# Attention and a three-way maxout layer on one core: two head pairs a turn, half-array matmuls in three stretches

## The chip, the core and the metric

The kernel runs on one core of a Trainium2 chip. The metric is the device time of one execution in microseconds (us). A core has a matmul engine (PE, with PEld for its weight loads), a vector engine (DVE), an activation engine (ACT), a general engine (POOL), and a queue engine (SP) that issues most DMAs. Each engine runs its own instructions in order and waits on semaphores for the others.

## What is computed

Inputs are q, k and v of 8 batches, 12 heads, 448 positions, 64 numbers a head, and four weights of 768 x 768, all float32.

```python
scores = scale * np.matmul(q, k.transpose(0, 1, 3, 2))     # scale = 1/8
m = np.max(scores, axis=-1, keepdims=True)
e = np.exp(scores - m)
attn = e / (np.sum(e, axis=-1, keepdims=True) + np.exp(-m) + 1e-09)
x = np.matmul(attn, v)                  # then (batch, position, head*64): 3584 x 768
h = np.maximum(np.maximum(x @ w1, x @ w2), x @ w3)
out = h @ w_out                         # 3584 x 768
```

The kernel leaves out the maximum m (it cancels): a row's weights are exp(score) over one plus their sum.

## The kernel before

Heads are worked on in pairs: NP = 48 pairs, NPAIR = 6 to a batch. The main loop (L452) does one pair an iteration, `p = it`, and finishes the pair before, `prev = it - 1`. P_DMA = 12 is the first pair of batch 2; from there the transposes of q and k are done by DMA instead of PE.

Of the 448 keys of a head, 384 are three chunks of 128 and 64 are left. The steps of a pair:

- `load` (L83): two DMAs (`q`, `k`, `v` each) from DRAM into one of NRAW = 3 raw buffers, each of HB = 3 pairs. They are issued on SP, as are DMA transposes and output stores, in program order.
- `cast_qk` (L165) on DVE to float16; `scale_v` (L191) on POOL; `transposes` (L204) into `qkT`, with an SP DMA from pair 12 on.
- `scores(p, c)` (L235): for chunk c, two matmuls with 64 rows, one for each head, each on one half of the PE array (tile `64*128`, side by side). Their result takes one of two buffers of the pool `ps_s`. `exp_scores` (L248) on ACT empties it. `scores_last` (L251) treats the 64 left keys of both heads in one full-array matmul, `exp_last` (L264) empties it into `eL`.
- `av_main` (L269): six full-array matmuls, `av_last` (L282): two half-array matmuls that end the sums. The results `avs` hold values and sums of weights, in the pool `ps_av` of two banks.
- `reciprocals` (L293) on ACT: two logarithms and one exponential. `normalize` (L302) on DVE for each head writes `xT` and frees an `av` bank.

When a batch has all six pairs normalized, `batch_done` (L435) appends its layer work to a queue: 18 `up` groups (six matmuls of 448 columns each, emptied by DVE into `hT`) and six or eight `op` groups (six matmuls of 384 columns, emptied by DVE into an output tile, one tile for two groups; three output tiles; stored by SP). `group()` (L443) takes one from the queue. Groups are spread between the attention steps; they use the pool `ps_u` of two banks. `n_groups` of 3 to 5 an iteration is worked out from the length of the queue.

There is no scheduler: the order written is the order on each engine (`manual_schedule`, L73). In an iteration from 12 on, before the change:

```python
cast_qk(it + 2); transposes(it + 2); scale_v(it + 1)
exp_scores(p, c, scores(p, c))                     # c = 0, 1
group()
avs = [av_main(prev, hh) for hh in range(2)]; av_last(prev, avs)
stp = scores(p, 2); stl = scores_last(p)
rb = reciprocals(prev, avs); exp_scores(p, 2, stp); exp_last(p, stl)
group(); normalize(prev, 0, avs, rb); group(); normalize(prev, 1, avs, rb)
...
load(it + 5, 1)
```

Batch 0 and 1 have orders of their own. Batch 0 fills PE with idle matmuls, and its weights (`load_weight`, L144) are loaded by POOL DMAs issued in iterations 3 to 8. In iterations 7 to 10, `casts(it + 1)` and PE transposes of the next pair stand inside the iteration.

Of the kernel before, what the change touches and what calls it, by code (L numbers as in the profile page):

```python
# [10 lines left out]
FP32 = mybir.dt.float32  # L11
FP16 = mybir.dt.float16
AF = mybir.ActivationFunctionType
# [8 lines left out]
def kernel(  # L22
# [11 lines left out]
    nc = tc.nc  # L34

    B, H, S, D = q.shape
    NTOK, DM = out.shape
    DFF = moe_w1.shape[1]
    NB = 3
# [24 lines left out]
    small = ctx.enter_context(tc.tile_pool(name="small", bufs=2))  # L64
    xt_pool = ctx.enter_context(tc.tile_pool(name="xt", bufs=2))
    ht_pool = ctx.enter_context(tc.tile_pool(name="ht", bufs=2))
    out_pool = ctx.enter_context(tc.tile_pool(name="outp", bufs=3))

    ps_s = ctx.enter_context(tc.tile_pool(name="ps_s", bufs=2, space=bass.MemoryType.PSUM))
    ps_av = ctx.enter_context(tc.tile_pool(name="ps_av", bufs=2, space=bass.MemoryType.PSUM))  # L70
# [2 lines left out]
    ctx.enter_context(tc.manual_schedule())  # L73


    NRAW = 3
    HB = NPAIR // 2
    raw = [
        [cpool.tile([128, 2 * HB, NB + 1, D], FP32, name=f"{n}in{i}") for n in "qkv"]
        for i in range(NRAW)  # L80
# [18 lines left out]
    load(1, 1, "qk")  # L99
    load(0, 1, "v")  # L100
    load(2, 1, "qk")
    load(1, 2, "v")
    load(3, 1, "qk")
    load(4, 2, "q")
    load(3, 1, "v")
    load(4, 2, "k")
    load(4, 2, "v")

# [4 lines left out]
    nc.vector.memset(raw[2][0][64:128, 0:2, NB, :], 0.0)  # L113
    load(NPAIR, 1, "qk")

    ident16 = cpool.tile([128, 128], MMDT, name="ident16")
# [34 lines left out]
    qkTs = {}  # L151
# [96 lines left out]
    def exp_scores(p, c, stp):  # L248
        nc.scalar.activation(out=eT[:, p % 2, c], in_=stp[:, :, 0:S], func=AF.Exp, scale=scale)  # L249

    def scores_last(p):  # L251

        stl = ps_s.tile([128, 2, 512], FP32, tag="s", name="stl")
        qkT, q0, k0 = qkTs.pop(p)
        nc.tensor.matmul(  # L255
            out=stl[:, 0, 0:S],
            lhsT=qkT[:, k0 + NB * 128 : k0 + NB * 128 + 128],
            rhs=qkT[:, q0 : q0 + S],
            start=True,
            stop=True,  # L260
        )
        return stl

    def exp_last(p, stl):  # L264
        nc.scalar.activation(out=eL[:, p % 2], in_=stl[:, 0, 0:S], func=AF.Exp, scale=scale)  # L265
# [177 lines left out]
    def group():  # L443
        if queue:
            queue.pop(0)()
# [3 lines left out]
    casts(0)  # L449
    transposes(0)  # L450
    keep_busy(3)
    for it in range(NP + 1):  # L452
        p = it if it < NP else None
# [12 lines left out]
        if it in (3, 4):  # L466
            load_weight(0, it - 3)
        if it in (5, 6, 8):
            load_weight((5, 6, 8).index(it) + 1)
        if it < NPAIR:  # L470

            casts(it + 1)
            for c in range(2):
                exp_scores(p, c, scores(p, c))
            if prev is None:
                keep_busy(3)
                exp_scores(p, 2, scores(p, 2))
                transposes(1)
                exp_last(p, scores_last(p))
            else:  # L480
                den, av = (ps_av.tile([128, 512], FP32, tag="av", name=n) for n in ("den", "av"))
                sums_main(prev, den, 1)
                stp = scores(p, 2)
                sums_main(prev, av, 0)
                stl = scores_last(p)
                sums_last(prev, den, 1)
                sums_last(prev, av, 0)
                exp_scores(p, 2, stp)
                exp_last(p, stl)
                rb = reciprocals_one(den)  # L490
                transposes(it + 1)
            if it < NPAIR - 1:
                keep_busy(3)
            else:

                ups = [up_open()]
                up_part(ups[0], 0, 0, 0, range(3))
                av5 = ps_s.tile([128, 2, 512], FP32, tag="s", name="av5")
                sums_main(p, av5[:, 1], 1)
                sums_main(p, av5[:, 0], 0)  # L500
                sums_last(p, av5[:, 1], 1)
                sums_last(p, av5[:, 0], 0)
                rb5 = reciprocals_one(av5[:, 1])
            if prev is not None:
                normalize_one(prev, av, rb)
            if it == NPAIR - 1:
                normalize_one(p, av5[:, 0], rb5)
                batch_done(0)
        elif it == NPAIR:
            exp_scores(p, 0, scores(p, 0))  # L510

            up_part(ups[0], 0, 0, 0, (3,))
            ups.append(up_open())
# [12 lines left out]
            exp_scores(p, 2, scores(p, 2))  # L526
            exp_last(p, scores_last(p))
            group()
            transposes(it + 1)
            group()  # L530
        else:
            late = it + 1 < P_DMA
            if not late:

                if it + 2 < NP:
                    cast_qk(it + 2)
                    transposes(it + 2)
                if it + 1 < NP:
                    scale_v(it + 1)
            if p is not None:  # L540
                for c in range(2):
                    exp_scores(p, c, scores(p, c))
# [5 lines left out]
            if p is not None:  # L548
                stp = scores(p, 2)
                stl = scores_last(p)  # L550
            rb = reciprocals(prev, avs)
            if p is not None:
                exp_scores(p, 2, stp)
                exp_last(p, stl)
# [6 lines left out]
            if it % NPAIR == 0:  # L561
                batch_done(prev // NPAIR)
# [41 lines left out]
```

## Time and profile before

| | |
|---|---|
| median of 3 runs | 367.58 us (367.43 to 367.74) |
| profiled execution | 367.07 us |
| its span, first to last instruction | 365.3 us |
| PE busy | 357.4 us, 98% |
| DVE busy | 243.4 us, 67% |
| ACT busy | 221.1 us, 61% |
| clock granted to PE | 0.999 of full |
| DMA moved | 58.61 MB, 160 GB/s on average |

The span is what the profile's times are counted in; the runs' time holds some 1.8 us more around it. PE's busy time is made of matmuls that overlap: one takes about 0.35 us from start to modelled end while the next starts 0.19 us after it. So what is read for PE is the distance from start to start. A timeline row names start, length, engine, line, operation, result and operands, the part of the array (128*128 or 64*128), the shape, and the count of equal instructions in a row; what stands in brackets is the idle time before it and who ended it.

### The profile page before, as it was taken

Reading aid. Unit: us, or ns where it says so; the run is one execution under the profiler, and the core shown is the slowest. Engines: PE = TensorE matmul, PEld = TensorE weight load, DVE = VectorE, ACT = ScalarE, POOL = GpSimd, SP = SyncE. Lnnn points to the kernel's source line nnn. Section 1 sums busy time; section 2 is a strip of 40 time slices with the busy share of each in tenths; the row PEclk is TensorE's granted clock in tenths of the full one; section 3 lists DMA queues with packets and bytes.
Section 4 is the critical chain, followed back from the end, with each engine's and each line's share of the span. In section 5 each row is a group of like instructions: output and inputs, shape, how many; then the busy total and the mean of one; then the engine's idle time right before and its main releaser. Section 6 shows DMA issues by size and latency. Waiting matters only on the chain.

```text
span 365.3 us, 6122 instructions
## 1 busy us (share of the span) xinstructions
PE 357.4 (98%) x2086; PEld 163.9 (45%) x2086; DVE 243.4 (67%) x521; ACT 221.1 (61%) x335; POOL 53.6 (15%) x159
## 2 busy tenths in 40 slices
PE   8999999999999999999999999999999999999995
PEld 3434444444444444444444444444444444445552
DVE  4474777876578677577657867757666776555553
ACT  4996476765666766666567666666566766651000
POOL 4263112211211211211121121121112112000000
PEclk9999999999999999999999999999999999999999
DMA  5999997668667888849764896758675673005006
GB/s 151 229 234 229 233 247 211 155 177 214 161 180 182 208 184 154 195 107 185 182 173 122 178 200 164 175 133 214 159 174 137 165 208 83 5 2 131 2 0 172
DMA packets 87951, 58.61 MB, mean 160 GB/s; under 512 B 43504, under 2 KB 84464, under 8 KB 87920
## 3 DMA queue, kind: packets, MB, share of 16 engines
q1 hardware_dynamic: 83632, 53.18, 59.7%
q0 software_dynamic: 3920, 4.72, 7.5%
q10 hardware_dynamic: 368, 0.33, 0.4%
q8 instruction: 16, 0.26, 0.3%
q14 instruction: 15, 0.12, 0.1%
HBM read 42.47 MB, written 11.01 MB: 146 GB/s over the span
## 4 chain that ended last, share of the span: by engine, by line
PE 91%; ACT 2%; DMA 2%; DVE 2%; issue 1%; SPq 0%; DVEq 0%
PE up L356 44%; PE op L390 15%; PE av L273 13%; PE stp L239 8%; PE stl L255 4%; PE av L285 3%; DMA kin<-in_k_dram 2%; PE busy L349 2%; ACT eT L249 1%; PE trT L221 1%; PE trT L226 1%; PE av L316 1%; DVE qkT L233 1%; DVE o_sb L415 0%; DVE qk L183 0%
## 5 line engine op out<-in xcount | busy, mean ns | idle before, releaser
L356 PE MATMUL up<-xT,w 128*128 128x448 f16 x864 | 175.3, 353 | 0.7 <-DVE xT L307 0.4
L249 ACT ACTIVATE eT<-stp 128x896 f16<-128x896 f32 x144 | 125.5, 910 | 53.3 <-PE stp L239 53.3
L356 PEld LDWEIGHTS <-w 128*128 128x128 f16 x864 | 81.7, 98 | 81.7 <-issue 12.5
L372 DVE TENSOR_TENSOR hT<-hT,up 128x448 f16<-128x448 f16 x96 | 59.6, 621 | 52.1 <-PE up L356 51.1
L157 POOL TENSOR_SCALAR vst<-vin 128x384 f16<-128x384 f32 x132 | 43.1, 338 | 255.2 <-issue 159.2
L298 ACT ACTIVATE lnd<-av 64x448 f32<-64x448 f32 x84 | 45.3, 539 | 49.0 <-PE av L285 48.0
L390 PE MATMUL op<-w,hT 128*128 128x384 f16 x336 | 59.3, 326 | 0.0
L273 PE MATMUL av<-eT,vst 128*128 128x448 f16 x252 | 54.5, 352 | 0.0
L307 DVE TENSOR_TENSOR xT<-av,rb 64x448 f16<-64x448 f32 x84 | 51.8, 617 | 1.4
L239 PE MATMUL stp<-qkT 64*128 64x448 f16 x288 | 44.1, 353 | 1.5 <-DVE qkT L233 0.7
L370 DVE CAST hT<-up 128x448 f16<-128x448 f32 x48 | 29.8, 624 | 22.9 <-PE up L356 22.2
L415 DVE TENSOR_SCALAR o_sb<-op 128x384 f32<-128x384 f32 (+1 forms) x56 | 30.8, 550 | 20.0 <-PE op L390 19.0
L390 PEld LDWEIGHTS <-hT 128*128 128x128 f16 x336 | 31.6, 98 | 24.7 <-issue 4.0
L273 PEld LDWEIGHTS <-vst 128*128 128x128 f16 x252 | 24.7, 98 | 22.4
L184 DVE CAST qk<-kin 128x384 f16<-128x384 f32 x47 | 25.7, 548 | 1.1 <-DMA kin<-in_k_dram 0.7
L265 ACT ACTIVATE eL<-stl 128x448 f16<-128x448 f32 x48 | 25.9, 539 | 0.0
L299 ACT ACTIVATE rb<-lnd 128x448 f32<-128x448 f32 x42 | 24.2, 576 | 1.3
L239 PEld LDWEIGHTS <-qkT 64*128 64x128 f16 x288 | 11.0, 94 | 23.2 <-issue 16.5
L419 ACT ACTIVATE o_sb<-op 128x192 f32<-128x192 f32 x1 | 0.3, 331 | 30.2 <-DVE o_sb L415 30.2
L189 DVE CAST qk<-kin 64x64 f16<-64x64 f32 x94 | 17.5, 187 | 1.3
L255 PE MATMUL stl<-qkT 128*128 128x448 f16 x48 | 17.4, 362 | 0.0
L285 PE MATMUL av<-eL,vst 64*128 64x448 f16 x84 | 15.2, 359 | 0.0
(50 smaller groups left out, 117.7 us busy)
## 6 DMA issues: line engine op xcount, KB each, us to landing
out_dram<-o_sb SPq DMA_DIRECT2D x54, 192.0 KB, 2.8
qin<-in_q_dram SPq DMA_DIRECT2D x46, 128.0 KB, 3.0
kin<-in_k_dram SPq DMA_DIRECT2D x45, 128.0 KB, 2.9
vin<-in_v_dram SPq DMA_DIRECT2D x44, 128.0 KB, 2.9
kin<-in_k_dram SPq DMA_DIRECT2D x46, 96.0 KB, 2.7
qin<-in_q_dram SPq DMA_DIRECT2D x45, 96.0 KB, 2.7
vin<-in_v_dram SPq DMA_DIRECT2D x44, 96.0 KB, 2.8
w<-in_moe_w_dram POOLq DMA_DIRECT2D x2, 1152.0 KB, 17.1
```

Source lines behind the costliest of these rows:

```text
L157: nc.gpsimd.tensor_scalar(out=out, in0=in_, scalar1=LAMBDA, scalar2=1.0, op0=ALU.mult, op1=ALU.mult)
L239: nc.tensor.matmul(out=stp[:, hh, 0:S], lhsT=qkT[hh * D : hh * D + D, k0 + c * 128 : k0 + c * 128 + 128], rhs=qkT[hh * D : hh * D + D, q0 ...
L249: nc.scalar.activation(out=eT[:, p % 2, c], in_=stp[:, :, 0:S], func=AF.Exp, scale=scale)
L255: nc.tensor.matmul(out=stl[:, 0, 0:S], lhsT=qkT[:, k0 + NB * 128 : k0 + NB * 128 + 128], rhs=qkT[:, q0 : q0 + S], start=True, stop=True,)
L273: nc.tensor.matmul(out=av[:, 0:S], lhsT=vst[:, p % VB, hh * NB + c, (1 - hh) * D : (3 - hh) * D], rhs=eT[:, p % 2, c, hh, :], start=(c == ...
L298: nc.scalar.activation(out=lnd[mine], in_=avs[hh][other, 0:S], func=AF.Ln, bias=1.0)
L307: nc.vector.tensor_tensor(out=xTs[b][mine, j, :], in0=avs[hh][mine, 0:S], in1=rb[mine], op=ALU.mult)
L356: nc.tensor.matmul(out=ps[:, 0:S], lhsT=w_sb[i][:, dc, ts(fc, 128)], rhs=xTs[b][:, dc, :], start=(dc == 0), stop=(dc == NDC - 1),)
L370: nc.vector.tensor_copy(out=h, in_=ps[:, 0:S])
L372: nc.vector.tensor_tensor(out=h, in0=h, in1=ps[:, 0:S], op=ALU.max)
L390: nc.tensor.matmul(out=ps[:, 0:NW], lhsT=hTs[sb][:, fc, ts(t, 128)], rhs=wout_sb[:, fc, ts(nh, NW)], start=(fc == 0), stop=(fc == NFC - 1),)
L415: nc.vector.tensor_scalar(out=o_sb[:, cs], in0=src, scalar1=1.0 / LAMBDA, scalar2=None, op0=ALU.mult)
```

## The change

Pairs 12 to 47 are done two a turn in a new loop; pairs 0 to 11 keep their iterations. In a turn, half-array matmuls stand in three stretches: `av_last(p-1)` with `scores(p, 0)` and `(p, 1)`; `scores(p, 2)` with `scores(p+1, 0)`; `av_last(p)` with `scores(p+1, 1)` and `(p+1, 2)`. The left keys of both pairs go into one `ps_s` buffer (`scores_last2`), emptied by one activation of 128 x 896 (`exp_last2`). `ready` casts, transposes and scales between the groups, twice a turn. Eight to ten groups are taken a turn.

Raw inputs have four buffers of two pairs; from pair 8 on they are loaded two pairs at a time, six DMAs a turn. For pairs 8 and 9 the load is issued in iteration 5, behind small memsets of the buffer. Output tiles are five. In the first loads, v of pair 1 goes alone and v of pairs 2 and 3 together.

```diff
-    out_pool = ctx.enter_context(tc.tile_pool(name="outp", bufs=3))
+    out_pool = ctx.enter_context(tc.tile_pool(name="outp", bufs=5))
...
-    NRAW = 3
-    HB = NPAIR // 2
+    NRAW = 4
+    HB = 2
...
-    load(1, 2, "v")
+    load(1, 1, "v")
     load(3, 1, "qk")
     load(4, 2, "q")
-    load(3, 1, "v")
+    load(2, 2, "v")
...
+    def scores_last2(p):
+        stl = ps_s.tile([128, 2, 512], FP32, tag="s", name="stl")
+        for n in range(2):
+            qkT, q0, k0 = qkTs[p + n]
+            nc.tensor.matmul(
+                out=stl[:, n, 0:S],
+                lhsT=qkT[:, k0 + NB * 128 : k0 + NB * 128 + 128],
+                rhs=qkT[:, q0 : q0 + S],
+                start=True,
+                stop=True,
+            )
+        return stl
+
+    def exp_last2(stl):
+        nc.scalar.activation(out=eL, in_=stl[:, :, 0:S], func=AF.Exp, scale=scale)
...
-    for it in range(NP + 1):
+    for it in range(P_DMA):
...
-        first = {3: 1, 4: 2}.get(it)
-        if first is not None:
-            hs = slice(2 * first, 2 * first + 2)
-            nc.vector.memset(raw[2][0][64:128, hs, NB - 1 : NB + 1, :], 0.0)
-            if first == 1:
-                load(NPAIR, 1, "v")
-            load(NPAIR + first, 1)
+        if it == 3:
+            nc.vector.memset(raw[NRAW - 1][0][64:128, 2:4, NB - 1 : NB + 1, :], 0.0)
+            load(NPAIR, 1, "v")
+            load(NPAIR + 1, 1)
+        if it == 5:
+            for t in raw[0]:
+                nc.vector.memset(t[64:128, :, NB - 1, 0:1], 0.0)
+            load(NPAIR + 2, 2)
...
-        for n in range(NPAIR + HB, 2 * NPAIR) if it == NPAIR else (it + 5,):
-            if it >= NPAIR and n < NP:
-                load(n, 1)
+        if it >= NPAIR and it % 2 == 0:
+            load(it + 4, 2)
+
+    def ready(p):
+        if p < NP:
+            cast_qk(p)
+            transposes(p)
+        if p - 1 < NP:
+            scale_v(p - 1)
+
+    avs = [av_main(P_DMA - 1, hh) for hh in range(2)]
+    for p in range(P_DMA, NP, 2):
+        left = max(len(queue) - LEFT, 0)
+        to_next = (NPAIR - p % NPAIR) // 2
+        n_groups = 8 if p % NPAIR == 0 else max(8, min(10, -(-left // to_next)))
+        av_last(p - 1, avs)
+        stps = [scores(p, c) for c in range(2)]
+        rb = reciprocals(p - 1, avs)
+        for c in range(2):
+            exp_scores(p, c, stps[c])
+        group()
+        normalize(p - 1, 0, avs, rb)
+        group()
+        normalize(p - 1, 1, avs, rb)
+        if p % NPAIR == 0:
+            batch_done(p // NPAIR - 1)
+        group()
+        exp_last2(scores_last2(p))
+        ready(p + 2)
+        for _ in range(n_groups - 7):
+            group()
+        stps = [scores(p, 2), scores(p + 1, 0)]
+        exp_scores(p, 2, stps[0])
+        exp_scores(p + 1, 0, stps[1])
+        group()
+        ready(p + 3)
+        if p + 4 < NP:
+            load(p + 4, 2)
+        avs = [av_main(p, hh) for hh in range(2)]
+        av_last(p, avs)
+        stps = [scores(p + 1, c) for c in (1, 2)]
+        rb = reciprocals(p, avs)
+        for c in (1, 2):
+            exp_scores(p + 1, c, stps[c - 1])
+        group()
+        for hh in range(2):
+            normalize(p, hh, avs, rb)
+        group()
+        group()
+        avs = [av_main(p + 1, hh) for hh in range(2)]
+    av_last(NP - 1, avs)
+    rb = reciprocals(NP - 1, avs)
+    group()
+    normalize(NP - 1, 0, avs, rb)
+    group()
+    normalize(NP - 1, 1, avs, rb)
+    batch_done(B - 1)
     while queue:
         group()
```

More of the change, by code (lines that the diff above doesn't have):

```diff
@@ L112 @@
         nc.vector.memset(raw[i][0][64:128, :, NB, :], 0.0)
-    nc.vector.memset(raw[2][0][64:128, 0:2, NB, :], 0.0)
+    nc.vector.memset(raw[NRAW - 1][0][64:128, 0:2, NB, :], 0.0)
     load(NPAIR, 1, "qk")
@@ L451 @@
     keep_busy(3)
-    for it in range(NP + 1):
-        p = it if it < NP else None
+    for it in range(P_DMA):
+        p = it
         prev = it - 1 if it > 0 else None
@@ L533 @@
             if not late:
[L535 to L542, printed above, removed]
+                cast_qk(it + 2)
+                transposes(it + 2)
+                scale_v(it + 1)
+            for c in range(2):
+                exp_scores(p, c, scores(p, c))
             group()
@@ L547 @@
             av_last(prev, avs)
-            if p is not None:
-                stp = scores(p, 2)
-                stl = scores_last(p)
+            stp = scores(p, 2)
+            stl = scores_last(p)
             rb = reciprocals(prev, avs)
-            if p is not None:
-                exp_scores(p, 2, stp)
-                exp_last(p, stl)
+            exp_scores(p, 2, stp)
+            exp_last(p, stl)
             if late:
@@ L560 @@
             normalize(prev, 1, avs, rb)
-            if it % NPAIR == 0:
-                batch_done(prev // NPAIR)
             if it + 2 == P_DMA:
@@ L567 @@
                 group()
-        for n in range(NPAIR + HB, 2 * NPAIR) if it == NPAIR else (it + 5,):
-            if it >= NPAIR and n < NP:
-                load(n, 1)
+        if it >= NPAIR and it % 2 == 0:
[14 more added lines that the diff above has]
+        rb = reciprocals(p - 1, avs)
+        for c in range(2):
+            exp_scores(p, c, stps[c])
[36 more added lines that the diff above has]
+    batch_done(B - 1)
     while queue:
```

## The prediction

> **What bounds the kernel.** I read the page's totals first, then busy time by stage, then the timeline of one pair on each engine, and the DMA answers for 28 to 50 us.
>
> Busy totals of the page:
>
> ```profile
> span 365.3 us, 6122 instructions
> PE 357.4 (98%) x2086; PEld 163.9 (45%) x2086; DVE 243.4 (67%) x521; ACT 221.1 (61%) x335; POOL 53.6 (15%) x159
> ```
>
> Stages, from pair 12 to pair 47 (columns: stretch, length, busy time by engine, clock, DMA):
>
> ```profile
> 73.10:323.00 249.90, 249.46 (x1414) 112.51 (x1415) 174.73 (x372) 163.81 (x248) 32.26 (x102) 1.00 0.68 162
> ```
>
> In this stage PE never lacks work: 249.46 of 249.90 us at full clock. A kernel can be shorter there only if the same matmuls take fewer start-to-start steps. One pair of heads on PE, from one `scores` to the next (start, length, name, count):
>
> ```profile
> 214.27 0.55 PE L239 MATMUL stp<-qkT 64*128 64x448 f16 x4
> 214.75 1.31 PE L356 MATMUL up<-xT,w 128*128 128x448 f16 x6
> 215.90 1.30 PE L273 MATMUL av<-eT,vst 128*128 128x448 f16 x6
> 217.13 0.36 PE L285 MATMUL av<-eL,vst 64*128 64x448 f16 x2
> 217.33 0.35 PE L239 MATMUL stp<-qkT 64*128 64x448 f16 x2
> 217.61 0.36 PE L255 MATMUL stl<-qkT 128*128 128x448 f16 x1
> 217.81 3.57 PE L356 MATMUL up<-xT,w 128*128 128x448 f16 x18
> 221.31 0.55 PE L239 MATMUL stp<-qkT 64*128 64x448 f16 x4
> ```
>
> The tail gives the plain step of a full-array matmul: 108 of them from 332.24 until the next kind starts at 352.78, 0.190 us each (0.189 without a 0.1 us stall among them):
>
> ```profile
> 332.24 20.70 PE L356 MATMUL up<-xT,w 128*128 128x448 f16 x108
> ```
>
> Two half-array matmuls (`64*128`) run side by side; two of `av` to two of `stp` is 217.13 to 217.33, 0.20 for a couple. The cycle is 7.04 us: 31 full matmuls make 5.86, four couples 0.80, and 0.38 is left for its two half-array stretches, 0.19 each. Locally: 18 `up` take 3.50 where 3.40 is due, 0.10 for entering; the `stp` x4 take 0.48 where 0.40 is due, 0.08 for leaving.
>
> **The change, part by part.**
>
> *Fewer stretches.* Two pairs had four stretches (`stp` x4; `av` x2 + `stp` x2; twice); a turn has three (6, 4 and 6 matmuls). Every matmul remains. Turns 12 to 46 are 18, so 18 stretches go: 18 x 0.19 = -3.4 us, all on PE, which bounds the stage. Ends: -3.2 (with 0.190 a step) and -3.6 (0.20 a stretch). The Trainium skill, "TensorEngine Tiling (Array Packing)", Key Properties, says that changing the tiling mode drains the array. A whole drain would be an estimate of 0.164 (a matmul's 353 ns less the 189 step) at both ends, 18 x 0.33 = 5.9; the row's 0.19 says the drain is partly covered, and I keep the row.
>
> *Old stalls that go.* At 80.17 the sixth `up` waits for batch 1's last normalize: due at 78.69 + 5 x 0.19 = 79.64, so 0.5 us. In turn 12 three `op` groups and the `stl` couple come before that `up`, which then starts 4.0 us after `av_last`, its sixth matmul at 4.9; normalize ends near 4.2. The `stp` at 73.10 take 0.73 instead of 0.48, a wait for ACT of 0.25 that goes too. Sum -0.75.
>
> *ScalarE inside a turn.* Its rows:
>
> ```profile
> 217.53 1.10 ACT L298 ACTIVATE lnd<-av 64x448 f32<-64x448 f32 x2 [1.13 <-PE av L285]
> 218.66 0.58 ACT L299 ACTIVATE rb<-lnd 128x448 f32<-128x448 f32 x1
> 219.15 0.90 ACT L249 ACTIVATE eT<-stp 128x896 f16<-128x896 f32 x1
> 219.94 0.54 ACT L265 ACTIVATE eL<-stl 128x448 f16<-128x448 f32 x1
> ```
>
> ACT starts 0.40 after `av_last`, needs 1.62 for the reciprocals, 0.80 a score tile, 0.90 to the end. With only two score buffers the tight place is the second stretch: its second couple needs `exp_last2` done. Counted from the turn's first `av_last`, with `op` groups (0.163 a matmul): three couples and leaving, 0.68; three groups, 3.62; `stl` couple, 4.00, its last result 4.16; group 4, 4.97; entering, 5.07; second couple at 5.27. `exp_last2` (taken as the 0.91 of the same 128x896 shape) starts 0.04 later and ends at 5.12, and PE sees it at 5.17: covered by 0.1; with `up` groups by 0.25. Before the third stretch and before `av_main(p+1)` the cover is 0.2 to 1 us. Price 0; if the cover fails, each 0.1 us is 1.8 us in all.
>
> *VectorE casts.* `ready` puts the casts of a pair between two group evacuations, in the middle of the turn. Rows of an odd batch:
>
> ```profile
> 215.21 0.55 DVE L178 CAST qk<-qin 128x384 f16<-128x384 f32 x1
> ...
> 216.51 0.40 DVE L189 CAST qk<-kin 64x64 f16<-64x64 f32 x2
> 216.94 0.62 DVE L370 CAST hT<-up 128x448 f16<-128x448 f32 x1
> ```
>
> 1.73 us (1.2 in an even batch, by the casts at 44.38). In a turn of `up` groups the second group's last result is out at 3.12; evacuation, normalize and evacuation follow at steps of 0.65, the third evacuation begins at 4.47, the casts run from 5.0 to 6.74, the fourth evacuation to 7.37. Its buffer is wanted at 9.2, so nothing stalls, except where group 5 is the first `op` after group 4, the last `up`: its sixth weight is wanted at 7.0, in turn 16, 0.5 us with the reload; and where two groups stand in the middle and an odd batch is cast (turns 28 and 40), 0.1 each. Sum +0.7 (0 to 1.5).
>
> *The switch at it = 11.* `av_main(11)` now follows directly on two `op` groups. DVE there:
>
> ```profile
> 72.47 0.60 DVE L307 TENSOR_TENSOR xT<-av,rb 64x448 f16<-64x448 f32 x1
> 73.17 0.56 DVE L415 TENSOR_SCALAR o_sb<-op 128x384 f32<-128x384 f32 x1
> 73.74 0.63 DVE L307 TENSOR_TENSOR xT<-av,rb 64x448 f16<-64x448 f32 x1
> ```
>
> Both `av` banks must be normalized first. PE arrives at 73.0 (first bank free 73.1) and 73.6 (second free 74.4): +0.9 once.
>
> *Loads.* SP issues 6 DMAs for two pairs instead of 12, at the same 0.6 us each (first two-pair loads of this kernel: 0.6 too); SP rows fall from 329 to 208. That costs nothing and frees SP; the transposes and stores behind them come sooner. In steady state the casts of pair p+3 end at 9.8 of the turn, a transpose (1.26 on SP) and four loads follow, the last k load is issued near 13 and cast at 13.9 + 5.8 = 19.7; two-pair loads landed in 4.0 to 5.0 us, so 1.7 us of cover. The memsets of `raw[0]` (three, some 0.1 us) and the fifth output tile (cover for stores that now queue behind six loads, 3.7 us) are off the path. On POOL three waits move. `scale_v(2)` waits for v of pairs 2 and 3 together (landed 18.5 before, as will be) and ends at 19.7, used by PE at 20.86; the first weight half behind it is issued 1 us later, lands near 28.5 and is used at 30.97. `scale_v(8)` waits for v of 8 and 9 (49.6, before 43.2); `av_main(8)` comes at 56.4. Behind it stands the load of w_out, issued 44.3 before, now near 50.7; with its 13.1 us it lands near 64, before the first `op` at 67.92. Pair 10's k then has less beside it, and comes some 3 us ahead of its cast.
>
> The place without cover is pair 8, in the stretch where weights load too:
>
> ```profile
> q0 software_dynamic: 2405, 3.10, 79.3%
> q1 hardware_dynamic: 2618, 2.10, 36.4%
> ```
>
> The SP queue (q1) lands one pair-load every 1.45 us there (issues at 37.52, 39.01, 40.39, 41.74 ...). Pair 8's k landed at 40.4 as the fourth of its loads; with q of pairs 8 and 9 ahead and both k's together it is the eighth: where q of pair 9 landed, 34.59 + 11.5 = 46.1. Its cast stood at 44.72, its transposes on PE at 45.78, and all later work of PE follows. If the queues share by descriptor (the two counts above are nearly equal), the eighth unit, with fewer completion descriptors, lands at 45.5 to 46.1, and PE stalls 0.6 to 1.2; I take 0.8 (0 to 2.5). Behind the waiting cast on DVE stand the two small casts, the copy of the transposes and the next group's evacuation, all of which PE waits for. The Trainium skill, "DMA: Bandwidth & Descriptors", Queues, rings and completion order, has each engine drain a whole packet (some 9 to 17 descriptors) of one queue before it switches. By that rule a doubled load gets a doubled turn, k lands near 42, this term is 0, and the second weight lands later, near its use at 42.5.
>
> Sum: -3.4 - 0.75 + 0.7 + 0.9 + 0.8 = -1.75. The profiled execution took 367.07 (span 365.3 and 1.8 around it), the median of the runs is 367.58; the change taken off the median gives 365.8 us.
>
> **The rivals.**
>
> *All covers hold.* Loads come in time and DVE keeps up: -3.4 - 0.75 and a little of the switch, 363.2 to 364.4. For it: 18 cycles without a stall in the stage. Against: the DVE rows at 73.74.
>
> *The score buffers stall every turn (slower).* Place: the second couple of the second stretch, waiting for `exp_last2`. Beyond its 0.1 to 0.25 cover each turn pays; from 0.1 us a turn the gain is gone (18 x 0.1 = 1.8), at 0.3 the time is 367.58 - 1.75 + 5.4 = 371.2. For it: two buffers, seven tiles a turn, and the stall of 73.10 was this wait. Against: the ACT rows repeat within 0.02 us.
>
> *Two-pair loads late (slower).* k would have to land 8 us after issue to pass the 1.7 us and then the 1.8 us that the fourth evacuation has spare; 8 to 11 us were seen only beside the weights. Each 0.2 us beyond costs 3 us in all; 370 or more.
>
> *The boundary is not saved.* No stretch of the stage had six matmuls; were the third couple to pay the 0.08 for leaving, 36 x 0.08 = 2.9 return, the result is 368.7. Against: the 12 half-array `av` at 31.63 take 1.33, 0.2 a couple to the end.
>
> **How the numbers follow.** No change can be told from one within 0.2%, some 0.7 us (366.8 to 368.3). Forecast with its once-only stalls, 364.6 to 366.8: 0.57. All covers hold: 0.17. Once-only stalls at their upper ends (-3.2 - 0.75 + 1.5 + 0.9 + 2.5 = +0.95 at worst): 0.11, most of it within 0.2%. Score buffers 0.07, late loads 0.04, boundary 0.04: slower. Faster 0.74, same 0.10, slower 0.16. The range 363.5 to 367.6 leaves out the slower cases and the lowest edge.
>
> **What will show it.** Right: three stretches a turn, a turn of 8 `up` groups near 13.88 us (before 14.08 for two pairs), PE idle before `av` near 73 and before `trT` near 46, no wait for xT near 80. Wrong: PE waits for ACT eL or for DMA kin in every turn, or couples slower than 0.20 in a long stretch.

## The result and the profile after

The changed kernel takes 370.06 us (median of 6 runs, 368.86 to 370.86); the kernel before, in the same series, 367.70 (367.43 to 367.89). The ratio is 1.0062 (95% interval 1.0050 to 1.0075): slower, where faster was forecast. The profiled execution took 370.10 us with a span of 367.9; before it was 367.07 and 365.3.

The page of the changed kernel, totals and the summary of the chain:

```profile
span 367.9 us, 5899 instructions
PE 354.7 (96%) x2086; PEld 167.5 (46%) x2086; DVE 245.3 (67%) x524; ACT 220.0 (60%) x317; POOL 54.3 (15%) x159
...
PE 83%; DVE 6%; SPq 4%; DMA 4%; issue 2%; ACT 1%; DVEq 0%
```

PE does the same 2086 matmuls in 2.7 us less of busy time, and the span is 2.6 us longer: PE idles more than the saving is worth. The chain says at what: 4% of it are SP's queue and 4% DMAs, in a kernel whose matmuls fill nearly all the rest.

By stage (stretch, length, then busy time of PE, PEld, DVE, ACT and POOL, clock, DMA share, GB/s; the first from the first `scores` of iteration 5 to turn 12, the second over the turns):

```profile
29.66:77.19 47.53, 46.44 (x298) 21.21 (x299) 33.69 (x75) 31.41 (x48) 9.38 (x26) 1.00 0.95 198
77.19:323.00 245.81, 242.28 (x1394) 114.10 (x1394) 175.14 (x369) 160.37 (x228) 32.80 (x102) 1.00 0.70 165
```

In the turns PE now lacks 3.53 us of work (245.81 less 242.28); before it lacked 0.44 in the like stage. And yet a turn is what it was meant to be. One turn of `up` groups on PE, changed kernel, from the second stretch on:

```profile
211.15 0.55 PE L239 MATMUL stp<-qkT 64*128 64x448 f16 x4
211.63 1.31 PE L373 MATMUL up<-xT,w 128*128 128x448 f16 x6
212.78 1.30 PE L290 MATMUL av<-eT,vst 128*128 128x448 f16 x6
214.01 0.36 PE L302 MATMUL av<-eL,vst 64*128 64x448 f16 x2
214.21 0.54 PE L239 MATMUL stp<-qkT 64*128 64x448 f16 x4
214.68 2.63 PE L373 MATMUL up<-xT,w 128*128 128x448 f16 x13
```

The third stretch has six half-array matmuls, 214.01 to 214.68, 0.67 us: three couples of 0.20 and 0.08 for leaving. Nothing in brackets: nothing waits. The turn of pair 20 with its 8 `up` groups takes 13.88 us, before 14.09. So the loss is outside the steady turns. I laid the starts of the same events of both profiles side by side:

| event | before | after | difference |
|---|---|---|---|
| first `scores` of iteration 5 | 27.58 | 29.66 | +2.08 |
| `av_last(10)` | 70.14 | 72.22 | +2.08 |
| last 108 `up` begin | 332.24 | 334.87 | +2.63 |
| from there to the end | 33.06 | 33.03 | -0.03 |

2.08 us are lost before iteration 5. From `av_last(10)` on, where 3.4 to 3.7 us are saved, 0.55 are lost net. Each loss has a row.

**The first loads.** PE and DVE of the changed kernel (start, length, operation; in brackets the idle time before it and what ended it):

```profile
22.21 0.39 PE L221 MATMUL trT<-ident,qk 128*128 128x128 f16 x4
...
24.06 0.55 PE L226 MATMUL trT<-ident,qk 128*128 128x128 f16 x4 [1.47 <-DVE qk L184]
```

```profile
23.45 0.55 DVE L184 CAST qk<-kin 128x384 f16<-128x384 f32 x1 [2.48 <-DMA kin<-in_k_dram]
```

The transposes of pair 4 wait for the cast of its k, and the cast waits for the load of k of pairs 4 and 5. That load was issued at 15.50 and 16.16 in both kernels; before, the transposes at 22.14 had no wait. The DMA part of the answers for these two issues, the kernel before and then the changed kernel:

```profile
DMA to landing us min/median/max: 4.1/4.5/5.0
```

```profile
DMA to landing us min/median/max: 7.1/7.1/7.2
```

They landed at 19.59 and 21.18 before, at 22.62 and 23.33 now. By the steps on PE this is 1.63 and 0.14 us. The other 0.3 arose at the very start, where the first `scores` matmul stands at 7.52 instead of 7.23; over the fourteen profiles of this case it starts anywhere from 6.82 to 7.67, so this part is scatter and not the change.

**The load of pairs 14 and 15.** PE of the changed kernel, first turn; then the chain of waits there; then SP's queue:

```profile
80.80 0.35 PE L269 MATMUL stl<-qkT 128*128 128x448 f16 x1
83.86 0.36 PE L269 MATMUL stl<-qkT 128*128 128x448 f16 x1 [2.71 <-DMA qkT<-qk]
84.06 1.30 PE L373 MATMUL up<-xT,w 128*128 128x448 f16 x6
```

```profile
77.64 6.17 DMA qkT<-qk
83.81 0.05 issue
83.86 0.36 PE stl L269
```

```profile
72.20 1.34 SPq L209 DMA_TRANSPOSE qkT<-qk  x1
73.59 0.60 SPq L92 DMA_DIRECT2D qin<-in_q_dram  x1
...
76.92 0.61 SPq L93 DMA_DIRECT2D vin<-in_v_dram  x1
77.64 1.25 SPq L209 DMA_TRANSPOSE qkT<-qk  x1
79.42 4.08 SPq L446 DMA_DIRECT2D out_dram<-o_sb  x6
```

`scores_last2(12)` takes the left keys of pairs 12 and 13 in one couple. The transposes of 12 were issued at 72.20. At the end of iteration 10 the code then says `load(14, 2)`: six issues of 0.59 to 0.61. Only behind them, at 77.64, the transposes of pair 13 go out, and they take 6.17 us to land behind the data of those loads. The second matmul of the couple, due at 81.0, stands until 83.86: 2.87 us by the steps. This alone is most of what the fewer stretches save.

The place on the queue is not new. The kernel before also had six load issues between the two transposes, for the one pair 15. SP there, and the landing of the second transpose:

```profile
70.11 1.35 SPq L209 DMA_TRANSPOSE qkT<-qk  x1
71.51 0.60 SPq L92 DMA_DIRECT2D qin<-in_q_dram  x1
...
74.80 1.38 SPq L93 DMA_DIRECT2D vin<-in_v_dram  x1
76.29 1.26 SPq L209 DMA_TRANSPOSE qkT<-qk  x1
```

```profile
DMA to landing us min/median/max: 2.9/2.9/2.9
```

It was issued 6.2 us after the first transpose, against 5.4 now, and landed in 2.91 us instead of 6.17. What changed is the size of the six loads, 1344 KB in all instead of 672 (256 and 192 KB an issue instead of 128 and 96), and that the turn wants the left keys of pair 13 together with those of pair 12. With a landing of 2.91 us they would have been there at 80.55, before 81.0.

**The rest**, by the steps on PE: 0.16 and 0.73 at the switch (75.21 and 76.51, `av` waiting for the normalize), 0.77, 0.22 and 0.13 in turns 16, 28 and 40, about 0.1 more in the tail; and 0.54 and 0.25 saved where old stalls went. With 18 stretches at the 0.205 us measured below, -3.7 - 0.8 + 2.87 + 0.9 + 1.1 + 0.1 = +0.5, against the 0.55 of the table.

### The profile page after: what moved, and what is told of

Read it like the earlier page. It is cut to its first block, busy times and chain, and to the rows that moved or that the text cites. A ratio compares the mean times of both kernels' runs of the same rounds, so it can differ in the third digit from the quotient of the medians.

```text
span 367.9 us, 5899 instructions
## 1 busy us (share of the span) xinstructions
PE 354.7 (96%) x2086; PEld 167.5 (46%) x2086; DVE 245.3 (67%) x524; ACT 220.0 (60%) x317; POOL 54.3 (15%) x159
## 4 chain that ended last, share of the span: by engine, by line
PE 83%; DVE 6%; SPq 4%; DMA 4%; issue 2%; ACT 1%; DVEq 0%
PE up L373 42%; PE op L407 13%; PE av L290 13%; PE stp L239 7%; PE av L302 3%; SPq L92 2%; DMA kin<-in_k_dram 2%; SPq L93 2%; DMA qkT<-qk 2%; PE stl L269 2%; DVE xT L324 1%; DVE hT L389 1%; DVE qk L184 1%; PE av L333 1%; PE stl L255 1%
## 5 line engine op out<-in xcount | busy, mean ns | idle before, releaser
L249 ACT ACTIVATE eT<-stp 128x896 f16<-128x896 f32 x144 | 123.6, 909 | 24.2 <-PE stp L239 24.2
L373 PEld LDWEIGHTS <-w 128*128 128x128 f16 x864 | 80.4, 98 | 86.6 <-issue 17.8
L315 ACT ACTIVATE lnd<-av 64x448 f32<-64x448 f32 x84 | 45.3, 539 | 63.2 <-PE av L302 62.2
L239 PE MATMUL stp<-qkT 64*128 64x448 f16 x288 | 40.8, 352 | 1.5 <-DVE qkT L233 0.7
L279 ACT ACTIVATE eL<-stl 128x896 f16<-128x896 f32 x18 | 16.5, 917 | 17.1 <-PE stl L269 17.1
L189 DVE CAST qk<-kin 64x64 f16<-64x64 f32 x94 | 21.7, 231 | 1.2
L239 PEld LDWEIGHTS <-qkT 64*128 64x128 f16 x288 | 12.8, 94 | 19.2 <-issue 11.7
L233 DVE COPY qkT<-trT 128x960 f16<-128x960 f16 x11 | 7.2, 657 | 10.8 <-PE trT L226 10.8
```

What stands on the lines that cost most here:

```text
L239: nc.tensor.matmul(out=stp[:, hh, 0:S], lhsT=qkT[hh * D : hh * D + D, k0 + c * 128 : k0 + c * 128 + 128], rhs=qkT[hh * D : hh * D + D, q0 ...
L315: nc.scalar.activation(out=lnd[mine], in_=avs[hh][other, 0:S], func=AF.Ln, bias=1.0)
L373: nc.tensor.matmul(out=ps[:, 0:S], lhsT=w_sb[i][:, dc, ts(fc, 128)], rhs=xTs[b][:, dc, :], start=(dc == 0), stop=(dc == NDC - 1),)
```

## The experiments

Two theories stood. **A**: the new turns save their 3.4 to 3.7 us, and the loss lies in two places where SP or the loads deliver late (k of pairs 4 and 5; transposes of pair 13). **B**: the turns themselves, or the two-pair loads, cost it. The parts were taken apart, the two places mended each by itself and together, then the remaining stalls.

### The turns alone: stretches

New turns, but the old raw buffers, one-pair loads, first loads and three output tiles.

```diff
-    out_pool = ctx.enter_context(tc.tile_pool(name="outp", bufs=5))
+    out_pool = ctx.enter_context(tc.tile_pool(name="outp", bufs=3))
...
-    NRAW = 4
-    HB = 2
+    NRAW = 3
+    HB = NPAIR // 2
...
-        if p + 4 < NP:
-            load(p + 4, 2)
+        for n in (p + 5, p + 6):
+            if n < NP:
+                load(n, 1)
```

> The new turns of two pairs with three half-array stretches alone; raw buffers, loads (one pair at a time, in the old order) and three output tiles stay as before. Theory A (each dropped stretch saves 0.19 us; the loss of the whole change comes from once-only waits, above all k of pairs 4 and 5 and the transposes of pair 13): -3.4 and -0.75 as forecast, the switch +0.9 and the op weights +1.1 remain, k of pair 4 in time again; 365.5 us, or about 1 more if the transposes of pair 13 still come late behind one pair's load. Theory B (the turn costs something in every round that the timeline hides, and the once-only waits only stand in its place): 367.7 us or more.

384.49 us against 367.54, ratio 1.0454 (1.0431 to 1.0476). PE has three waits of over 4 us, at 128.28, 218.10 and 307.16. The first, on PE, DVE and SP of this kernel:

```profile
128.28 2.40 PE L373 MATMUL up<-xT,w 128*128 128x448 f16 x6 [4.52 <-DVE o_sb L432]
```

```profile
127.67 0.56 DVE L432 TENSOR_SCALAR o_sb<-op 128x384 f32<-128x384 f32 x1 [5.33 <-DMA out_dram<-o_sb]
```

```profile
123.41 0.60 SPq L93 DMA_DIRECT2D vin<-in_v_dram  x1
124.11 3.75 SPq L446 DMA_DIRECT2D out_dram<-o_sb  x6
```

With three tiles the evacuation of an `op` waits for a store, and the stores stand behind twelve load issues that a turn makes in one go. PE waits for that evacuation. The six `up` after it take 2.40 us instead of 1.30: their steps are 0.373, and the clock granted in that stretch is 0.50. The turns can't be had with these loads and three tiles. The time lies in theory B's open range (367.7 or more), but these three waits make it, so this kernel says nothing yet on the turns themselves. One thing it does show: the transpose of pair 13, issued behind six one-pair loads, landed in 3.62 us, and the couple of left keys waited 0.30 us at 79.53.

### The loads alone: loads

The old loop over all iterations, with the new buffers, the new loads and five output tiles.

```diff
-        for n in range(NPAIR + HB, 2 * NPAIR) if it == NPAIR else (it + 5,):
-            if it >= NPAIR and n < NP:
-                load(n, 1)
+        if it >= NPAIR and it % 2 == 0 and it + 4 < NP:
+            load(it + 4, 2)
```

> The other half of the change alone: raw inputs in four buffers of two pairs, loaded two pairs at a time, and five output tiles, in the old loop of one pair an iteration with its four stretches for two pairs. Theory A (the new loads cost PE once near 24 us, because v of pair 1 alone leaves the queue short early and k of pairs 4 and 5 lands later; nothing else): +1.3 to +1.9, 369.0 to 369.6 us; the transposes of pair 13 come late too but are wanted only near 82 there, so at most 0.5 more. Theory B (loads of two pairs disturb every iteration by their bursts): 371 us or more, with waits for DMA spread over the span.

372.78 us against 367.46, ratio 1.0160 (1.0102 to 1.0217). `av_last(10)` starts at 72.12, so the 2 us of the first loads are in this kernel as well: they don't come from the turns. Then the load of pairs 14 and 15 is late, in another way. DVE of this kernel:

```profile
78.00 0.43 DVE L183 CAST qk<-qin 128x512 f16<-128x512 f32 x1 [1.65 <-DMA qin<-in_q_dram]
...
81.86 0.55 DVE L184 CAST qk<-kin 128x384 f16<-128x384 f32 x1 [3.43 <-DMA kin<-in_k_dram]
```

Behind that cast stands the evacuation that PE waits for at 83.36 (3.67 us by the steps). The load was issued at 73.5 to 77.5 in both kernels; in the changed one the casts of pair 14 come at 81.99 and 82.34 and find their data, in the old loop DVE is ready for them at 76.35, over 5 us sooner. So the old loop has no cover for the two-pair loads at this place. The time is in theory B's range (the four runs took 371.43 to 376.35), but the waits that it expected over the whole span are not there: from `av_last(13)` to `av_last(45)` this kernel takes 224.62 us, the kernel before 224.38. In the steady state the two-pair loads cost next to nothing; the loss is at their start.

### The turns with five output tiles: stretches5

The kernel of the turns alone, with `bufs=5` for the output tiles.

> The new turns with the old raw buffers and one-pair loads, and five output tiles instead of three. Theory A (the three waits of 4 to 5 us of the run with three tiles, and the half clock after them, come from an evacuation that waits for a store which stands behind twelve loads on SP, and from nothing else): they go, 365.0 to 366.0 us. Theory C (twelve load issues a turn leave SP too little time, so that stores or transposes come late whatever the tiles): 368 us or more.

367.65 us against 367.46, ratio 1.0003 (0.9987 to 1.0019), between the two forecasts. The three long waits are gone: two tiles more took 16.8 us off (384.49 to 367.65). What is left are waits of PE for the transposes, 0.29 to 0.91 us, in five of the places I looked at (79.86, 90.32, 133.13, 217.04, 305.33): SP has twelve load issues a turn where two-pair loads need six. The turns do better with the two-pair loads (`moved14` below takes 366.18), for SP's sake. The transpose of pair 13 landed in 3.62 us here too, and cost 0.29.

### Two output tiles less: tiles3

The kernel `moved14` of below, with three output tiles.

> The whole change with the load of pairs 14 and 15 ahead, and three output tiles instead of five. Theory A (five tiles are needed whenever stores stand behind a turn's loads on SP; six issues are 3.9 us instead of twelve with 7.8): an evacuation waits for a store in turns 16, 28 and 40, 0.5 to 3 us each, none longer; 367.5 to 372 us. Theory B (tiles mattered only beside twelve issues): 366.2 us.

375.43 us against 367.49, ratio 1.0230 (1.0183 to 1.0276); with five tiles it is 366.18. That is more than theory A's 367.5 to 372. DVE of this kernel:

```profile
127.82 0.56 DVE L432 TENSOR_SCALAR o_sb<-op 128x384 f32<-128x384 f32 x1 [3.19 <-DMA out_dram<-o_sb]
```

PE waits 2.45, 1.78 and 1.95 us for such evacuations. The store is queued behind six loads. Behind the first of these waits the granted clock is 0.50 for 3.4 us, and so it is after PE's wait near 24 us, where the tiles have no part: 1.45 us of the 8.6 between the profiled executions had arisen before `av_last(10)`. So the fourth and fifth tile are worth some 7 us here, not the whole 9 between the medians; I had put the fifth "off the path", which it is only as long as it is there.

### The first loads, one-pair v: early

```diff
     load(1, 1, "v")
+    load(2, 1, "v")
     load(3, 1, "qk")
     load(4, 2, "q")
-    load(2, 2, "v")
+    load(3, 1, "v")
     load(4, 2, "k")
```

> The whole change, but the first loads in the order that feeds k of pairs 4 and 5 as early as before: v of pairs 1 and 2 go singly right after q and k of pair 2, v of pair 3 after q of pairs 4 and 5. Theory A: the wait of 1.6 us on PE near 24 us goes or shrinks below 0.5; since later work comes 1.6 us sooner, k of pair 8 (landed 45.4, wanted at 46.8) may now be waited for by up to 0.5; time 368.3 to 369.0 us. Theory B (nothing is gained by an earlier start, since the loads that follow set the pace): no change from 370.1 us.

370.42 us against 367.54, ratio 1.0078 (1.0063 to 1.0093): nothing gained. Two issues more put k of pairs 4 and 5 at 16.77 and 17.43; it landed at 21.62 and 22.39, one us sooner, and PE still waited 1.39. As that wait shrank, one of 0.37 us for pair 8 appeared at 47.16. The wait for pair 13 stayed, 2.34 us by the steps; PE of this kernel:

```profile
82.78 0.36 PE L270 MATMUL stl<-qkT 128*128 128x448 f16 x1 [2.18 <-DMA qkT<-qk]
82.98 2.30 PE L374 MATMUL up<-xT,w 128*128 128x448 f16 x6
```

Here the six `up` after the wait run at half clock (2.30 us; the granted clock is 0.50), and the steps stay at 0.373 to about 86.5. By an estimate from these steps, 3.4 us at half clock cost PE 1.7 us of its work.

### The load of 14 and 15 moved: moved14

```diff
-        if it >= NPAIR and it % 2 == 0:
-            load(it + 4, 2)
+        if it in (6, 8, 9):
+            load({6: 10, 8: 12, 9: 14}[it], 2)
```

The load of pairs 14 and 15 goes ahead of the transposes of pair 12 instead of between those of 12 and 13.

> The whole change, but the load of pairs 14 and 15 is issued at the end of iteration 9 instead of 10, ahead of the transposes of pair 12 instead of between those of 12 and 13. Theory A: the transposes of pair 13 are then issued about 73.6 us and land near 77, before the second stl matmul near 81, so its 2.9 us wait goes; 367.2 us. Theory B: the transposes land late because DMA is short of capacity there, and the wait moves to another transfer; 369 us or more.

366.18 us against 367.54, ratio 0.9962 (0.9948 to 0.9977): 3.9 us faster than the changed kernel (3.7 when each is taken against the runs of before in its own series), and faster than before; theory A had said 367.2. SP and PE of this kernel:

```profile
71.94 3.11 SPq L209 DMA_TRANSPOSE qkT<-qk  x2
75.16 7.66 SPq L446 DMA_DIRECT2D out_dram<-o_sb  x6
```

```profile
80.51 0.54 PE L269 MATMUL stl<-qkT 128*128 128x448 f16 x2
80.89 1.30 PE L373 MATMUL up<-xT,w 128*128 128x448 f16 x6
```

Both transposes go out one behind the other, each lands in 2.8 us, the second instead of 6.17, and the couple has no wait. The edit moves one load and no matmul. That gives theory A its larger half.

### Both: both

The edits of `early` and `moved14` together.

> Both of these edits together on the whole change. Theory A: the two savings add up, 1.6 and 2.9 less up to 0.5 for k of pair 8; 365.5 to 366.2 us, faster than before by 0.4 to 0.6%. Theory B: 368 us or more.

366.49 us against 367.54, ratio 0.9972 (0.9962 to 0.9982), not distinguishable from `moved14` alone, and just above theory A's 365.5 to 366.2. PE waited at 24.03 again, 1.87 us by the steps, although v goes by single pairs: the way to mend the first loads was wrong. The first loads are those of `early`, yet k of pairs 4 and 5 landed at 22.52 and 23.30, as in the changed kernel. With the first loads of the changed kernel, too, the wait is not always the same: 1.63 there and in `loads`, 1.32 in `moved14`, 1.87 in `split14`, 1.92 in `tiles3`. So `early`'s one us sooner is within the scatter.

### The first loads, fewer issues: early23

On `moved14`, q and k of pairs 2 and 3 as two-pair loads, so that four issues fewer stand ahead of k of pairs 4 and 5.

```diff
-    load(2, 1, "qk")
+    load(2, 2, "q")
+    load(2, 2, "k")
     load(1, 1, "v")
-    load(3, 1, "qk")
     load(4, 2, "q")
```

> The whole change with the load of pairs 14 and 15 ahead (366.18 us before), and q and k of pairs 2 and 3 in loads of two pairs, so that the first loads take four DMAs fewer. In the run with single v loads the first DMAs landed a constant 2.5 to 2.8 us after their issue until 13 us, so the queue had nothing waiting and the 0.65 us an issue on SP set the pace. Theory A (k of pairs 4 and 5 is late because the early DMAs carry too little each): it lands 1 us or more sooner than 23.0 us, the wait of 1.3 to 1.9 us near 24 us shrinks below 0.5; 364.8 to 365.5 us. Theory B (the transfers themselves are the limit there): no change, 366.2 us.

365.38 us against 367.49, ratio 0.9940 (0.9926 to 0.9955). k of pairs 4 and 5 was issued at 12.94 and 13.60 and landed at 19.12 and 19.97; PE's wait near 24 is gone. A smaller one came at the start, since k of pair 2 now lands with pair 3's:

```profile
13.87 0.34 PE L226 MATMUL trT<-ident,qk 128*128 128x128 f16 x3 [0.58 <-DVE qk L184]
```

`av_last(10)` starts at 70.63 instead of 72.22. That is theory A's other half, but for the 0.5 us to 70.14.

All fourteen profiles sort by their first loads. From the first `scores` matmul to `av_last(10)` it takes 62.9 to 63.5 us with those of before, 64.7 to 65.0 with those of the changed kernel and of `early` (66.3 in the two where the clock halves after the wait), and 63.2 to 63.8 with those of `early23`. The DMA rate in the second of a page's 40 slices goes the same way: 226 to 235, 191 to 203, and 235 to 243 GB/s. Pair 8's k, too, landed sooner in `early23` (42.90 instead of 45.39), and its cast had no wait.

### One stretch more in each turn: split14

On `moved14`, one group between `scores(p, 0)` and `scores(p, 1)`: four stretches in a turn, as two pairs had before.

```diff
-        stps = [scores(p, c) for c in range(2)]
+        stps = [scores(p, 0)]
         rb = reciprocals(p - 1, avs)
-        for c in range(2):
-            exp_scores(p, c, stps[c])
+        exp_scores(p, 0, stps[0])
         group()
+        stps.append(scores(p, 1))
+        exp_scores(p, 1, stps[1])
```

> The whole change with the load of pairs 14 and 15 ahead (366.18 us in the first comparison), and in every turn one group of full-array matmuls put between scores(p, 0) and scores(p, 1): four stretches a turn again, the same matmuls. It measures the boundary by itself. Theory A: 18 stretches more at 0.19 us, +3.4; 369.6 us. Theory B (the stretches are free, the gain of the first comparison came from elsewhere): 366.2 us.

369.90 us, ratio 1.0076 (1.0051 to 1.0101) to a before of 367.46: 3.7 more than `moved14`, which ran beside another set of runs of before (367.54). PE of this kernel, first stretches of a turn:

```profile
205.76 0.36 PE L302 MATMUL av<-eL,vst 64*128 64x448 f16 x2
205.96 0.35 PE L239 MATMUL stp<-qkT 64*128 64x448 f16 x2
206.24 1.15 PE L407 MATMUL op<-w,hT 128*128 128x384 f16 x6
207.32 0.36 PE L239 MATMUL stp<-qkT 64*128 64x448 f16 x2
207.62 2.12 PE L407 MATMUL op<-w,hT 128*128 128x384 f16 x12
```

The turn of pair 20 takes 14.09 us instead of 13.88, and from `av_last(13)` to `av_last(45)`, 16 turns, it is 226.39 instead of 223.11 us: 3.28 / 16 = 0.205 per stretch. The turns without any wait are 0.21 to 0.22 longer each. The saving is there in full, 18 x 0.205 = 3.7 us, and theory B falls. (The profiled execution, 371.71 us, is the slowest of the four: after PE's wait near 24 us, 1.71 us of it idle, its granted clock is 0.50 for 3.4 us. The stretch measured lies behind that, and the other three took 369.53 to 370.00.)

### A combination that failed: best

The turns with five tiles and one-pair loads (`stretches5`), the second normalize of iteration 11 ahead of the group, and the casts of p+2 behind the middle groups in every turn.

```diff
-            group()
-            normalize(prev, 1, avs, rb)
+            if it + 1 == P_DMA:
+                normalize(prev, 1, avs, rb)
+                group()
+            else:
+                group()
+                normalize(prev, 1, avs, rb)
...
-        ready(p + 2)
         for _ in range(n_groups - 7):
             group()
+        ready(p + 2)
```

> The kernel of the run before with two orders mended: in iteration 11 both normalizes come before the third group's evacuation on DVE, and in a turn the casts of pair p+2 come after the middle groups. Theory A: the 0.9 us before av_main(11) shrink to below 0.2, the waits of op for hT in turns 16, 28 and 40 (0.4, 0.2 to 0.4, 0.1 to 0.3) go; 363.6 to 364.6 us, 0.8 to 1.1% faster than before. Theory C: later casts delay the transposes of pair p+2, which PE then waits for in the next turn; no gain over the run before.

378.31 us, ratio 1.0298 (1.0269 to 1.0326); theory A's forecast for it fell. The wait at iteration 11 did go, but PE now waited 1.19 to 3.32 us for transposes, at 79.89, 135.02, 221.81, 265.85 and 310.96, and 0.5 at two more places. SP of this kernel, ahead of the second of them:

```profile
124.63 0.60 SPq L93 DMA_DIRECT2D vin<-in_v_dram  x1
125.33 5.13 SPq L446 DMA_DIRECT2D out_dram<-o_sb  x8
130.57 3.28 SPq L209 DMA_TRANSPOSE qkT<-qk  x2
133.90 0.67 SPq L92 DMA_DIRECT2D qin<-in_q_dram  x1
```

Casting later moves the transposes behind the stores of those groups on SP. What helps DVE is paid on SP where SP has no slack.

### The small stalls: final and final2

`final` is `early23` with the second normalize of iteration 11 ahead of the group (the first part of the diff above).

> The kernel of the run before, and in iteration 11 both normalizes ahead of the third group's evacuation. Theory A (the wait before av_main(11) is DVE's order alone): 0.7 to 0.9 less, 364.0 to 364.7 us, 0.8 to 0.95% faster than before the change. Theory B: the evacuation that now comes later is waited for by the next group instead; no gain.

364.85 us against 367.49, ratio 0.9926 (0.9911 to 0.9941), just above theory A's range. Of the 0.73 and 0.16 at the switch 0.10 and 0.16 are left, without a wait for the normalize; 0.5 came back in turns 16, 28 and 40, where PE now loses 0.47, 0.33 and 0.35 on `hT` (in `early23` 0.40, 0.09 and 0.17).

`final2` casts p+2 behind the middle groups in those three turns alone.

```diff
-        ready(p + 2)
+        late_casts = p % (2 * NPAIR) == 4
+        if not late_casts:
+            ready(p + 2)
         for _ in range(n_groups - 7):
             group()
+        if late_casts:
+            ready(p + 2)
```

> The kernel of the run before, and in turns 16, 28 and 40, where an op group follows the last up, the casts of pair p+2 after the middle groups. Theory A: the waits of op for hT (0.4, 0.2 and 0.2) go, 0.5 to 0.8 less; 363.4 to 364.0 us. Theory C (casts and so transposes that come 1.2 us later are waited for in the next turn, as where every turn had them so and SP issued twelve loads): slower by 1 us or more than the run before.

364.47 us against 367.49, ratio 0.9914 (0.9900 to 0.9929): the fastest version, 0.86% below before, though 0.5 us above the forecast. The page:

```profile
span 362.3 us, 5895 instructions
PE 354.2 (98%) x2086; PEld 167.3 (46%) x2086; DVE 245.4 (68%) x524; ACT 220.0 (61%) x317; POOL 53.9 (15%) x159
```

PE is at 98% again, with the smaller busy time. The waits of `op` for `hT` are gone; one of 0.38 us at 127.87, of an `up` for the evacuation of a buffer by DVE, is new.

## Why the prediction was wrong

**The step that failed first: "That costs nothing and frees SP; the transposes and stores behind them come sooner."** The issues did fall, from 371 DMAs on SP to 251, and in the steady turns, where `ready` issues both transposes of a turn ahead of its load, the step holds. It was never followed through at the one place where a load stands between two transposes, the end of iteration 10. I counted issues, and by issues that place had not got worse: six stand there before and after. What a transpose behind loads waits for is their data as well. Behind six one-pair loads it landed in 2.91 us (before; 3.62 in `stretches` and `stretches5`, where the couple waited 0.3), behind six two-pair loads in 6.17, behind none in 2.8 (`moved14`). Nor has the prediction a row for when the keys of pair 13 are first wanted: `scores_last2(12)` takes them one couple before the turn's second stretch. The sum put this at nothing, and it cost 2.87 us; `moved14` moved that one load and was 3.7 to 3.9 us faster. The 0.8 to 1.0 us more is not fully explained. `moved14` also waits 0.3 less near 24, and a half clock behind the wait, as `early` shows it, may be in some runs of the changed kernel: the three whose mean granted clock was 0.992 or 0.993 took 370.02 to 370.86 us, the three at 0.998 to 1.000 took 368.86 to 370.10.

**The second: the first loads.** I asked of the moved v only who waits for v. What changed was the traffic ahead of k of pairs 4 and 5: the DMAs moved 201 GB/s instead of 229 in the second of the page's 40 slices. As I read it, an issue takes 0.65 us whether it carries one pair or two, so v of one pair alone (112 KB an issue on average) leaves the engines short just then, and the rest of the bytes still lies ahead of k. That reading is borne out as far as it goes: `early`, with more issues, gained nothing, `early23`, with four fewer, removed the wait, and the fourteen profiles sort by it. That the issues and not some other trait of the order set the pace was not tested by itself. It cost 1.8 us here, 2.08 with the scatter of the start; counted from the first `scores`, `early23` took back 0.9 in its profile, and `final` and `final2` with the same first loads 1.5.

**The steps that held.**
- Fewer stretches, -3.4 (-3.2 to -3.6): 0.205 each, -3.7. The row's 0.19 was a little low, and the whole drain of 0.33 (the Trainium skill, "TensorEngine Tiling (Array Packing)", Key Properties: a switch of mode drains the array) is not what a stretch costs: it would have given 5.9.
- Old stalls, -0.75: 0.54 and 0.25 went.
- ScalarE at price 0: no turn of the profile shows PE waiting for ACT; `exp_last2` took 0.92 us, 0.91 was assumed.
- VectorE casts, +0.7 (0.5, 0.1, 0.1): 0.77, 0.22, 0.13 in the three turns named.
- The switch at iteration 11, +0.9: 0.73 and 0.16.
- `scale_v(2)`, the weights and w_out: no wait of PE on them in the profile.

**Pair 8, +0.8, was right in mechanism and paid nothing.** The two-pair loads beside the weights landed at 36.33, 39.97, 42.88 and 45.39: about 3 us each, twice the 1.45 of a one-pair load, and k at 45.39 where 45.5 to 46.1 was said. But all of PE was 2 us late by then, by a loss that the prediction had not seen, and the cast at 46.80 had its data. That the term cost nothing is luck:

```profile
46.80 0.55 DVE L184 CAST qk<-kin 128x384 f16<-128x384 f32 x1
```

In `early`, with a smaller delay before, 0.37 us of the stall were there. The packets of the two queues from 36 to 41 us were equal, 483 each (507 and 508 before):

```profile
q0 software_dynamic: 483, 0.74, 81.1%
q1 hardware_dynamic: 483, 0.41, 32.0%
```

The shares stayed one to one when the loads doubled, so a doubled load did not get a doubled turn. That was how I had read the rule of the Trainium skill that I weighed against the row ("DMA: Bandwidth & Descriptors", Queues, rings and completion order: an engine drains a whole packet of one queue before it switches), and by that reading k would have landed near 42. How large the packets of that rule are here, no run shows.

**The rivals.** None of the four came true: no stall in every turn, no k load late in the turns, and the boundary was saved. The slower outcome was a fifth, a wait for DMA transposes behind larger loads on SP, and the list lacked it, though the queue of SP was among the things the edit visibly changed. Without the two missed terms the measured ones sum to -3.7 - 0.8 + 1.1 + 0.9 + 0.1 = -2.4 us, where -1.75 was forecast (with 0.8 for pair 8); with both places mended and most of the 1.1 and 0.9 gone, `final2` is 3.0 us below before.

## What to carry to other kernels

When loads are made larger and fewer, don't only count the issues: write down the order of every queue they stand in, with the bytes that go ahead of each transfer, for the first round and the switch as well as for the steady loop, and for each transfer behind a moved load ask when its reader first wants it. Buffers that look idle in one order (the fourth and fifth output tile) can be what the next order lives on. And a cover has to be found on every engine the moved work passes: `best` gained on VectorE and lost more on SP.

## What the runs showed of the hardware

- An issue on SP's queue that waited for nothing took about 0.6 us (0.59 to 0.68) for one pair and for two, a DMA transpose 1.23 to 1.35. Where little is under way, at 8 to 13 us of `early`, DMAs landed a flat 2.5 to 2.8 us after issue, and came at the pace of the issues, one in 0.65 us.
- A DMA transpose landed in 2.8 us behind nothing (`moved14`), in 2.9 to 3.6 behind six one-pair loads on the same queue (before, `stretches`, `stretches5`, `best`) and in 6.17 behind six two-pair loads.
- After an idle time of PE the granted clock can fall to 0.50 and the steps double, to 0.373 us, for 3.4 us each time and once for 6.8. So it was after the idle times of 4.0 to 4.5 us (`stretches`), of 3.51 (`loads`) and of 2.18 (`early`), while after the 2.71 us of the changed kernel the steps were 0.19 at once (six `up` at 84.06 in 1.30 us). In `best` alone, 2.73 us (at 221.81) and 2.31 (at 310.96) were followed by half clock, 3.16 (at 135.02) was not. How long an idle time it takes was not settled.
